# A later down product, three sums pinned to VectorE, and one level instead of two in one more chunk: an attention and expert kernel on one Trainium2 core

## The chip, the cores and the metric

The program runs on one core of a Trainium2 chip. The metric is the time of one execution on the device in microseconds; lower is better. Before the change it is 1823.2 us (median of 3 runs, 1819.77 to 1824.88). The granted clock is the share of its full clock that TensorE was given, 1.00 at most. "PE" is TensorE, "DVE" VectorE, "ACT" ScalarE, "POOL" GpSimd, "SP" the engine that issues most transfers here (580 of the 692 that the trace of the kernel before lists; POOL issues the rest).

## The reference, cut to what matters

```python
kv  = np.einsum('bhsd,bhse->bhde', k, v)            # linear attention, 8 batches, 8 heads
out = np.einsum('bhsd,bhde->bhse', q, kv)
x   = (out / rms(out) * g_norm)                     # reshaped to 4608 rows x 512
p   = probs / (probs.sum(-1, keepdims=True) + 1e-9)
for e in range(4):                                  # four experts
    h = np.maximum(x @ w1[e], 0.0)                  # "up":   512 -> 1024
    out += p[:, e:e+1] * (h @ w2[e])                # "down": 1024 -> 512
```

All in fp32. The four experts are the four passes of the kernel; each pass goes over nine chunks of 512 rows. I count passes from 0 and chunks of the whole program from 0 to 35, so chunk 9 is the first of pass 1.

## The kernel before

The products use a scheme with 7 instead of 8 block products. The up product applies it twice (7 x 7 small products of 128 columns). The down product applies it once (256 columns, `down`) or twice (128 columns, `down_deep`): fewer multiplications, but sums before and after on DVE and POOL. A planner in the kernel's own Python takes every operation with a cost it was given, a key that says how early it is wanted, and the buffers it needs, and lays down the order of each engine; the program that runs follows that order.

```python
def either(n):                       # the planner may choose DVE or POOL
    return {"DVE": 0.17 + 0.00108 * n, "POOL": 0.1 + 0.0025 * n}
...                                  # cut
SHAPE = {"big": (29, 2 * NT), ...}   # 29 buffers of 4 KB a partition, and 4 more later
...                                  # cut: in up(), as the inner products end, hidden forms h[..]
            elif m == 7:
                add(key, made[1], made[1], made[7])
                add(key, unit(4), made[1], made[5])
                relu(key, h[4])
                add(key, unit(5), h[21], h[4])
                add(key, unit(6), h[5], h[1], ALU.subtract)
...                                  # cut: up's PSUM banks are emptied by
nc.vector.tensor_tensor(out=block(whole, a, t), in0=src.ap[:, 0:HN], in1=add_.ap[:], op=ALU.add)
...                                  # cut: second-level sums of w2, 28 of 256 columns a pass
combine(deep + j / 7, either(HN), parts[o][1], parts[a][1], parts[b][1], op, ...)
...                                  # cut: down and down_deep
        h = hidden.pop(s)
        base = s + 1.0               # when the down product of chunk s is wanted
...
            if e and 1 <= c < NCH - 1:   # e: pass, c: chunk in the pass, NCH = 9
                down_deep(s, e, c)
            else:
                down(s, e, c)
```

PSUM banks are the buffers that this program's matmuls write to. In the profile, L802 is the up matmul, L966 the one-level and L1039 the two-level down matmul. L826 is the sum that empties an up bank, L1072 the same for a two-level down bank. L337 is every sum and difference from SBUF to SBUF on DVE or POOL, L1100 a sum of two-level down products, L936 the output transfer that adds into memory. "big", "small", "kv", "x_rem" and "kvbd" are names of buffers that the planner gives out; for most purposes they are one store.

## Time and profile before

| | before |
|---|---|
| median time | 1823.2 us (later rounds 1820 to 1822) |
| span in the profile | 1817.9 us |
| PE matmul instructions | 14390: 7056 up, 4116 two-level down, 1680 one-level down, rest attention |
| busy PE / DVE / POOL | 97 / 67 / 60% |

The prediction below shows the lines that carry the argument. I add two groups of L337, the 1024-column sums on DVE and on POOL (out and in shapes, count, then total busy us and mean ns):

```profile
L337 DVE TENSOR_TENSOR big<-big,big 128x1024 f32<-128x1024 f32 x238 | 340.0, 1431 | 32.7 <-ACT big L785 25.2 <-POOL big L337 1.3 <-issue 1.0
L337 POOL TENSOR_TENSOR big<-big,big 128x1024 f32<-128x1024 f32 x97 | 238.8, 2468 | 92.5 <-DVE big L826 27.4 <-PE db L966 18.2 <-ACT big L785 13.7
```

PE is the bound, so what counts is where PE does not run back to back. I measured that as a **loss**: over all neighbouring matmuls, the distance from start to start beyond 0.1116 us (128 columns) or 0.2164 us (256 columns), summed by chunk. The loss includes a lower granted clock: in the kernel before it was 0.50 from 952.2 us on for 3.41 us, and matmuls of 128 columns started 0.213 us apart there. It can be checked from a window: its length less its own matmuls. Before, chunks 8 to 35 lose 62.7 us in all.

### The profile page before, as it was taken

The page shows a single profiled execution, that of the slowest core. Times are in us where ns is not written, and L with a number is a line of the kernel's source. Part 1 is how long each engine was busy: PE and PEld are TensorE (multiplying, and loading weights), DVE is VectorE, ACT ScalarE, POOL GpSimd, SP SyncE. Part 2 cuts the span into 40 slices and gives each one's busy share as a digit, 9 for nine tenths or more (in the row PEclk, how much of TensorE's full clock was granted, in tenths as well). Part 3 has the DMA queues.
Part 4 walks back from the last instruction along what each step waited for, and adds up shares of the span by engine and source line. Part 5 has one row for each costly group of instructions (what it writes and reads, how often), then busy time and mean ns, then how long its engine had stood idle before and what let it go on. Part 6 is the DMA issues. An engine that isn't in the chain of part 4 may idle for free.

```text
span 1817.9 us, 36718 instructions
## 1 busy us (share of the span) xinstructions
PE 1764.0 (97%) x14390; PEld 1693.5 (93%) x14390; DVE 1211.4 (67%) x1929; ACT 825.7 (45%) x1961; POOL 1085.7 (60%) x898
## 2 busy tenths in 40 slices
PE   8999999999999999999989999999998999999998
PEld 8899999999999999999988899999997899999997
DVE  4755565556565667677777667777777666777774
ACT  3544444454333345554443344545443344445452
POOL 4975544546554556666565566666655756675752
PEclk9899999999999999999999999999999999999999
DMA  9844453533433444444544434444445434444442
GB/s 228 247 154 148 136 164 125 148 105 116 157 128 105 105 101 106 116 105 110 150 109 108 102 98 104 106 109 107 129 140 118 99 95 108 105 106 105 105 105 47
DMA packets 148589, 220.83 MB, mean 121 GB/s; under 512 B 49600, under 2 KB 90816, under 8 KB 148416
## 3 DMA queue, kind: packets, MB, share of 16 engines
q1 hardware_dynamic: 133312, 191.21, 33.7%
q0 software_dynamic: 15104, 27.27, 10.9%
q8 instruction: 113, 1.85, 0.4%
q14 instruction: 60, 0.49, 0.1%
HBM read 145.30 MB, written 73.14 MB: 120 GB/s over the span
## 4 chain that ended last, share of the span: by engine, by line
PE 88%; DVE 7%; issue 2%; POOL 1%; DMA 1%; ACT 0%; SPq 0%; DVEq 0%; POOLq 0%
PE u L802 41%; PE db L966 16%; PE db L1039 13%; PE ab L1039 10%; DVE big L337 4%; PE ab L966 3%; PE ab L595 1%; DVE big L1100 1%; PE ab L577 1%; DVE big L826 1%; PE ab L562 1%; PE ab L605 1%; PE u L1164 1%; DMA out_dram<-big 0%; DVE small L1100 0%
## 5 line engine op out<-in xcount | busy, mean ns | idle before, releaser
L802 PE MATMUL u<-xf,big 128*128 128x128 f32 x3456 | 481.9, 278 | 11.9 <-DVE big L337 7.2
L802 PEld LDWEIGHTS u<-xf,big 128*128 128x128 f32 x3456 | 440.8, 194 | 22.6 <-ACT snap L818 6.9
L826 DVE TENSOR_TENSOR big<-u,snap 128x256 f32<-128x256 f32 x696 | 286.7, 420 | 249.2 <-PE u L802 152.6
L337 DVE TENSOR_TENSOR big<-big,big 128x1024 f32<-128x1024 f32 (+1 forms) x359 | 425.2, 1197 | 32.7 <-ACT big L785 25.2
L818 ACT ACTIVATE snap<-u 128x256 f32<-128x256 f32 x756 | 287.9, 382 | 310.0 <-PE u L802 227.5
L337 POOL TENSOR_TENSOR big<-big,big 128x256 f32<-128x256 f32 (+1 forms) x206 | 329.8, 1610 | 152.4 <-DVE big L337 54.9
L802 PE MATMUL u<-xf,w1y 128*128 128x128 f32 x2700 | 377.5, 277 | 19.5 <-DVE big L826 15.7
L802 PEld LDWEIGHTS u<-xf,w1y 128*128 128x128 f32 x2700 | 339.8, 192 | 27.2 <-DVE big L826 20.1
L966 PE MATMUL db<-big,big 128*128 128x256 f32 x1256 | 297.3, 381 | 7.6 <-DVE big L337 7.6
L966 PEld LDWEIGHTS db<-big,big 128*128 128x128 f32 x1256 | 228.9, 191 | 34.0 <-DVE big L337 8.4
L1064 ACT ACTIVATE snap<-db 128x256 f32<-128x256 f32 x252 | 89.4, 356 | 173.6 <-PE db L1039 166.4
L337 POOL TENSOR_TENSOR big<-big 128x512 f32<-128x512 f32 (+1 forms) x91 | 142.3, 1564 | 43.0 <-ACT big L785 31.3
L936 POOL DMA_DIRECT2D out_dram<-big x102 | 91.6, 1005 | 118.9 <-ACT big L913 66.2
L785 ACT ACTIVATE big<-big 128x1024 f32<-128x1024 f32 x130 | 136.7, 1051 | 26.5 <-DVE big L337 26.4
L1072 DVE TENSOR_TENSOR big<-ab,snap 128x256 f32<-128x256 f32 (+1 forms) x216 | 82.9, 384 | 94.9 <-PE ab L1039 67.5
L818 ACT ACTIVATE big<-u 128x256 f32<-128x256 f32 x232 | 88.5, 382 | 103.7 <-PE u L802 100.6
L1039 PE MATMUL db<-big,big 128*128 128x128 f32 x820 | 113.3, 276 | 0.4 <-DVE big L337 0.4
L913 ACT ACTIVATE big<-db,p_all 128x256 f32<-128x256 f32 x88 | 41.6, 473 | 136.5 <-PE db L966 136.3
L1039 PEld LDWEIGHTS db<-big,big 128*128 128x128 f32 x820 | 102.0, 192 | 0.7 <-DVE big L337 0.6
L1039 PE MATMUL ab<-kv,big 128*128 128x128 f32 x608 | 87.2, 275 | 0.0
L1039 PE MATMUL db<-kv,big 128*128 128x128 f32 x600 | 84.8, 275 | 0.0
L920 DVE SCALAR_TENSOR_TENSOR big<-db,p_all,big 128x256 f32<-128x256 f32 x70 | 33.8, 483 | 74.6 <-PE db L966 73.3
(200 smaller groups left out, 2665.7 us busy)
## 6 DMA issues: line engine op xcount, KB each, us to landing
xf<-x SPq DMA_DIRECT2D x108, 512.0 KB, 3.6
out_dram<-big POOLq DMA_DIRECT2D x86, 256.0 KB, 5.3
xf<-x_h SPq DMA_DIRECT2D x81, 256.0 KB, 3.0
xf<-x SPq DMA_DIRECT2D x81, 256.0 KB, 3.4
x<-xf SPq DMA_DIRECT2D x36, 512.0 KB, 3.2
big<-in_moe_w_dram SPq DMA_DIRECT2D x27, 512.0 KB, 6.9
small<-in_q_dram SPq DMA_DIRECT2D x72, 128.0 KB, 3.6
kv<-in_k_dram SPq DMA_DIRECT2D x30, 288.0 KB, 3.3
```

The costliest lines, as they stand in the source:

```text
L337: lambda eng: adder(eng).tensor_tensor(out=out_(), in0=a(), in1=b(), op=op),
L785: lambda eng: nc.scalar.activation(out=b.ap[:], in_=b.ap[:], func=ACT.Relu),
L802: nc.tensor.matmul(ps.ap[:, u * P:(u + 1) * P], lhsT=w1f[e][m][mm][1]()[:, u * P:(u + 1) * P], rhs=views[m][mm][1](), start=(mm in (1, 2, ...
L818: lambda eng: nc.scalar.activation(out=where(), in_=ps.ap[:, 0:HN], func=ACT.Copy),
L826: lambda eng: nc.vector.tensor_tensor(out=block(whole, a, t), in0=src.ap[:, 0:HN], in1=add_.ap[:], op=ALU.add),
L913: lambda eng: nc.scalar.activation(out=cell(i, half), in_=ap(), func=ACT.Copy, scale=prob()),
L920: lambda eng: nc.vector.scalar_tensor_tensor(out=cell(i, half), in0=ap(), scalar=prob(), in1=cell(i, half), op0=ALU.mult, op1=ALU.add,),
L936: nc.gpsimd.dma_start(out=dst, in_=cell(i)[parts, :], accum_op=ALU.add)
L966: nc.tensor.matmul(ps.ap[:, 0:HN], lhsT=four(h[m])[:, kt // 2, t, kt % 2, :], rhs=w2f[e][m].ap[:, kt * HN:(kt + 1) * HN], start=(m in (1, ...
L1039: nc.tensor.matmul(ps.ap[:, o * P:(o + 1) * P], lhsT=b.ap[:, col:col + P], rhs=w2q[e][m][mm][1]()[:, kt, :], start=(mm in (1, 2, 5) and o ...
L1064: lambda eng: nc.scalar.activation(out=where(), in_=group_of(ps.ap), func=ACT.Copy),
L1072: lambda eng: nc.vector.tensor_tensor(out=cell(tq, dq), in0=group_of(src.ap), in1=group_of(add_.ap), op=ALU.add,),
```

## The change

Intent: give the sums between an up and its down product more time, keep the last of these sums off the slower engine (a 1024-column sum took 2.47 us on average on POOL, 1.22 undisturbed on DVE), and relieve DVE and POOL of two-level work in the last two chunks of a pass, when the next pass's weights are being summed.

```diff
-        def add(key, to, a, b, op=ALU.add):
+        def add(key, to, a, b, op=ALU.add, where=either):
...
-                add(key, unit(4), made[1], made[5])
+                add(key, unit(4), made[1], made[5], where=dve)
                 relu(key, h[4])
-                add(key, unit(5), h[21], h[4])
-                add(key, unit(6), h[5], h[1], ALU.subtract)
+                add(key, unit(5), h[21], h[4], where=dve)
+                add(key, unit(6), h[5], h[1], ALU.subtract, dve)
...
-        base = s + 1.0                       # in down and in down_deep
+        base = s + 1.2
...
-            if e and 1 <= c < NCH - 1:
+            if e and 1 <= c < NCH - 2:
```

I call the three parts the sums, the trail and the level.

More of the change, by code (lines that the diff above doesn't have):

```diff
@@ L774, in up @@
         h = {}
-        def add(key, to, a, b, op=ALU.add):
+        def add(key, to, a, b, op=ALU.add, where=either):
             combine(
-                key, either(2 * NT), lambda: to.ap[:], lambda: a.ap[:], lambda: b.ap[:], op,
+                key, where(2 * NT), lambda: to.ap[:], lambda: a.ap[:], lambda: b.ap[:], op,
                 [a, b], [to],
@@ L992, in down_deep @@
         h = hidden.pop(s)
-        base = s + 1.0
+        base = s + 1.2
         merge, send = result(s, e, c, base)
```

## The prediction

Passages of the recorded text are cut, as marked: they told of the hardware what no run here shows. No term of the forecast was in them; its sum is -22.9 us, which gives the 1800. The times in ns are those of one sum (L337).

> **What bounds the kernel now.** I read the page first, then the chain of waits, then a table of stretches cut at the chunk borders, then the timeline where that table shows lost time. The page:
>
> ```profile
> PE 1764.0 (97%) x14390; PEld 1693.5 (93%) x14390; DVE 1211.4 (67%) x1929; ACT 825.7 (45%) x1961; POOL 1085.7 (60%) x898
> ...
> PE 88%; DVE 7%; issue 2%; POOL 1%; DMA 1%; ACT 0%; SPq 0%; DVEq 0%; POOLq 0%
> ```
>
> TensorE is the bound: 97% busy, 88% of the chain. A change can win only in the 7% that the chain gives to VectorE, and must pay for every matmul it adds. To place the 7%, I cut the span where each chunk's first up product starts (196 up matmuls a chunk, 36 chunks, four passes of nine; passes counted from 0). Columns: window; its length; busy us and count of PE, PEld, DVE, ACT, POOL; granted clock; DMA share; GB/s.
>
> ```profile
> 485.60:532.10 46.50, 46.35 (x309) 43.10 (x309) 26.48 (x45) 16.99 (x39) 28.86 (x20) 1.00 0.47 156
> 532.10:579.90 47.80, 46.57 (x309) 43.31 (x308) 31.54 (x45) 17.56 (x40) 19.90 (x14) 1.00 0.33 100
> 579.90:626.70 46.80, 44.68 (x302) 41.78 (x302) 29.76 (x37) 17.67 (x41) 24.81 (x28) 1.00 0.36 96
> ```
>
> ```profile
> 671.00:714.80 43.80, 43.80 (x395) 43.80 (x394) 31.71 (x54) 22.61 (x56) 28.11 (x23) 1.00 0.41 106
> ...
> 894.00:942.60 48.60, 46.16 (x399) 45.19 (x398) 35.48 (x59) 21.40 (x54) 29.12 (x24) 1.00 0.46 136
> 942.60:999.50 56.90, 50.73 (x318) 46.30 (x317) 40.51 (x59) 21.08 (x47) 34.17 (x27) 0.97 0.49 115
> 999.50:1046.50 47.00, 44.67 (x302) 41.78 (x302) 28.50 (x38) 16.89 (x40) 27.09 (x30) 1.00 0.41 102
> ...
> 1090.40:1136.00 45.60, 44.21 (x390) 43.63 (x389) 34.28 (x55) 22.28 (x56) 30.19 (x22) 1.00 0.44 104
> 1136.00:1180.20 44.20, 44.20 (x398) 44.20 (x397) 32.33 (x55) 22.77 (x57) 28.35 (x23) 1.00 0.41 105
> ```
>
> The second fence is quoted from the stretches of passes 1 and 2; the first is the end of pass 0. In the trace, matmuls of 128 columns follow each other every 0.1116 us (1.79 us for 16), those of 256 columns every 0.2164 us (3.46 for 16). So an up product is 196 x 0.1116 = 21.9 us, a two-level down product 196 x 0.1116 = 21.9, a one-level one 112 x 0.2164 = 24.2. Whatever a window has beyond its own matmuls is lost. The loss is 0.0 in 671 to 714.8 and 2.3 in 1090 to 1136; such pairs alternate through passes 2 and 3. Around the change of weights, the three chunks from the pass's last on lose 3.5 + 10.0 + 2.5 = 16.0 us (894 to 1046.5) and the same places one pass later 16.1. The end of pass 0, where every down product is one-level already, loses 0.4 + 1.7 + 2.3 = 4.4. That contrast carries my prediction. What holds PE in the worst chunk:
>
> ```profile
> 946.73 2.58 DVE L337 TENSOR_TENSOR big<-big,big 128x1024 f32<-128x1024 f32 x1
> ...
> 952.78 1.22 DVE L337 TENSOR_TENSOR big<-big,big 128x1024 f32<-128x1024 f32 x1
> ...
> 961.35 3.15 DVE L337 TENSOR_TENSOR big<-big,big 128x1024 f32<-128x1024 f32 x1
> ```
>
> ```profile
> 943.56 4.67 POOL L337 TENSOR_TENSOR big<-big,big 128x1024 f32<-128x1024 f32 x2
> ...
> 961.06 2.36 POOL L337 TENSOR_TENSOR big<-big,big 128x1024 f32<-128x1024 f32 x1 [1.12 <-DVE big L826]
> ```
>
> The same add takes 1.22 us when POOL rests and 2.58 or 3.15 when POOL adds at that time; a PSUM bank's evacuation stands behind it, and PE needs the bank. Last, the end of the kernel:
>
> ```profile
> 1785.02 2.96 DVE big L337 x2
> 1787.98 0.04 issue
> 1788.02 12.31 PE db L966 x48
> ```
>
> The last down product needs two chained sums (its forms 5 and 6), and PE, with nothing else left, stands for 3.56 us.
>
> [...]2468 ns mean on POOL, 1216 ns undisturbed on DVE, for 1024 columns.[...] the granted clock is 0.97 in the 56.9 us chunk and 0.94 in its twin one pass later[...].
>
> **The change part by part.**
>
> (a) One level for the last-but-one chunk of passes 1 to 3. It removes 3 x 196 matmuls of 128 columns and adds 3 x 112 of 256: 3 x (24.24 - 21.87) = +7.1 us, all on the path. It removes, per chunk, for DVE and POOL together: 7 differences of 512 columns, 14 of 256, 7 sums of 512, and 9 evacuation sums of 256 with 3 of 128. At the undisturbed DVE times in the trace (0.68, 0.41, 0.68, 0.42, 0.29) that is 4.8 + 5.7 + 4.8 + 3.8 + 0.9 = 20 us. One-level output has 6 accumulating merges of 0.48 us on DVE, 2.9 us, the other 8 on ACT at 0.47 us, which has room. Net some 17 us of DVE and POOL work leave the stretch just before the weight sums of the next pass (DVE plus POOL: 64.6 us in 894 to 942.6, 74.7 in the next), and 11 of the 4 KB buffers are no longer asked for, so weights can land and be summed sooner. If passes 1 and 2 then ended like pass 0, (16.0 - 4.4) + (16.1 - 4.4) = 23.3 us would return. I count three quarters of it, 17.5, because the trailing down product keeps eight hidden forms longer just where both sets of weights need the buffers, and because the 2.5 us loss of the chunk where the second-level weights are summed stays in pass 0's case too.
>
> (b) The down product a fifth of a chunk later. It adds no instruction, and no PE time. It gives the chain behind the up outputs (sum, ReLU, sum, difference) 0.2 x 45 = 9 us more. At the end it leaves PE about 0.2 x 24.2 = 4.8 us of the former down product to do after the last up product, more than the 3.56 us hole. That last stretch also ran at a clock of 0.91 after its hole; the whole loss from 1738 us on is 5.5 us. I count 4.5 back.
>
> (c) Three sums a chunk on DVE only. Of the eleven 1024-column sums of a steady two-level chunk POOL makes 3 to 5 now; in the chunks I placed by hand, one or two of them are among these three. So about 1.5 x 1.22 = 1.8 us more DVE work a chunk of 44 (32 to 35 busy now), some 3.7 us less on POOL, and fewer collisions, unless the planner gives POOL other sums. All two-level chunks of steady state together lose 20.6 us now (5.3, 7.7 and 7.6 in passes 1 to 3). With (b) I count 8 of these, less than half: those waits are PSUM evacuations behind a sum that collided, and neither part removes the other sums on POOL.
>
> Pass 0 I leave as it is: its steady chunks are 59.6 us of back-to-back matmuls with no loss.
>
> Sum: +7.1 - 17.5 - 4.5 - 8 = -22.9 us. From 1823.2 that gives about 1800; **1800 us predicted**, 1.3% less.
>
> **The rivals.** First, the buffers: hidden forms that live longer push the weight loads later, and new waits on loads or on w1 sums take the place of the removed ones. For it: the loads already trickle in pairs between 870 and 953 us, as room comes. Against it: part (a) frees eleven. Then only the final hole is won and the net is near 0: 1818 to 1828. Second, PE pays 7.1 us and the collisions only move: the schedule is made by a planner that takes fixed durations, so each new order has its own bad coincidences. For it: the same kind of chunk loses 0.0 in one place and 2.3 in the next. Against it: pass 0's end is the same code and loses 4.4. This gives 1805 to 1815. Third, everything works: pass ends like pass 0 (-23.3), end hole closed (-5.5), steady losses down to 6 (-14.6), +7.1, so -36.3: 1787, just at the 2% line. DVE as the new bound I think unlikely: below 36 of 44 us in steady chunks.
>
> **Range and chances.** The middle of these is 1800; 8 times in 10 between 1784 and 1816. Faster by over 2% needs below 1786.7, the third rival's full size: 0.13. Slower by over 2% needs +36 us, five times the added matmuls, with a bound engine that otherwise does the same work: 0.02. Within 2%: 0.85.
>
> **What would show it.** Step (a): the windows of the last chunks of passes 1 and 2 hold 112 matmuls of 256 columns, and the chunk after loses under 5 us instead of 10, at a granted clock of 1.00; the weight loads start earlier than 870. Step (b): no wait of 3.56 us before the last down product. Step (c): no 1024-column sum of forms 4, 5, 6 on POOL, POOL busy under 1085.7 us, steady pairs of chunks under 89.8 us. I am wrong if the chunks at the change of passes still lose 8 us or more, or if steady chunks lose more than 1.1 us on average, which is what they lose now.

## The result, and the profile after

The changed kernel takes 1795.13 us (median of 4 runs, 1793.68 to 1795.63) against 1821.49 us of the kernel before in the same rounds (4 runs). The ratio is 0.9852, 95% interval 0.9834 to 0.9871. (Ratios here are the mean time of one kernel's runs over that of the other's of the same rounds, so not quite the ratio of the medians.) That is 1.5% faster; 1800 was predicted.

The page after, span, busy time and the chain by engine:

```profile
span 1793.0 us, 36253 instructions
...
PE 1760.0 (98%) x14138; PEld 1683.6 (94%) x14138; DVE 1177.1 (66%) x1909; ACT 815.9 (46%) x1913; POOL 973.0 (54%) x816
...
PE 84%; POOL 5%; DMA 5%; DVE 3%; issue 2%; ACT 1%; SPq 1%; DVEq 0%; POOLq 0%; ACTq 0%
```

DVE fell from 7 to 3% of the chain. Something new stands there: POOL and DMA, 5% each. I come back to it. The stretches after, cut the same way (window, length, busy us and count of PE, PEld, DVE, ACT, POOL, clock, DMA share, GB/s): the second chunk of pass 1 (in the second chunk of each later pass w2's second-level sums are made), the three chunks at the change from pass 1 to 2, and two steady chunks.

```profile
576.10:625.30 49.20, 46.28 (x303) 42.95 (x302) 32.00 (x46) 19.03 (x41) 27.56 (x29) 0.97 0.36 97
891.00:938.60 47.60, 46.98 (x331) 44.31 (x331) 35.62 (x57) 21.37 (x51) 24.96 (x23) 1.00 0.65 171
938.60:986.30 47.70, 47.70 (x317) 44.63 (x316) 23.40 (x37) 17.47 (x40) 28.35 (x21) 1.00 0.47 117
986.30:1035.60 49.30, 46.25 (x301) 43.12 (x301) 33.36 (x42) 18.47 (x40) 26.71 (x33) 0.97 0.37 96
1078.80:1123.90 45.10, 44.27 (x395) 43.98 (x395) 33.10 (x55) 22.94 (x57) 28.49 (x21) 1.00 0.42 106
1123.90:1168.50 44.60, 44.22 (x395) 43.94 (x394) 33.09 (x55) 22.89 (x57) 28.44 (x21) 1.00 0.45 107
```

The chunk of 56.9 us has become one of 47.7 in which PE never stops. The chunk after it, 47.0 us before, has become worse: 49.3. The two steady chunks last 89.7 us together, as good as unchanged from 89.8. The end of the kernel, in the chain:

```profile
1763.83 12.09 PE db L966 x56
1775.91 12.10 PE ab L966 x56
```

The hole of 3.56 us in front of the last down product is gone.

**The losses of all runs.** us lost on PE; "end 0" are chunks 8 to 10, "end 1" 17 to 19, "end 2" 26 to 28 (last chunk of a pass and the two after it); "border" is the sum over the third and eighth chunk of passes 1 to 3, "inner" over the four between them; "last" is chunk 35 with the tail. "Median" and ratio are timed; losses are of the one profiled run.

| kernel | median us | ratio (95%) | end 0 | end 1 | end 2 | border | inner | last |
|---|---|---|---|---|---|---|---|---|
| before | 1821 | 1 | 4.4 | 16.0 | 16.1 | 9.4 | 11.2 | 5.5 |
| the change | 1795.1 | 0.9852 (.9834-.9871) | 9.1 | 5.7 | 5.7 | 1.9 | 11.4 | 0 |
| level | 1805.2 | 0.9905 (.9889-.9922) | 6.1 | 7.9 | 6.3 | 5.9 | 11.2 | 5.8 |
| trail, passes 1-3 | 1811.6 | 0.9939 (.9919-.9959) | 2.1 | 16.1 | 15.9 | 1.4 | 14.1 | 1.0 |
| sums 4 and 6 | 1805.0 | 0.9905 (.9882-.9928) | 2.9 | 15.0 | 15.3 | 2.8 | 8.1 | 7.9 |
| trail (1-3) + level | 1804.7 | 0.9902 (.9887-.9917) | 2.0 | 11.3 | 10.2 | 4.1 | 14.4 | 0 |
| trail + sums | 1813.8 | 0.9956 (.9941-.9971) | 9.1 | 15.2 | 15.3 | 2.5 | 13.8 | 2.7 |
| level + sums 4, 6 | 1790.8 | 0.9837 (.9820-.9855) | 2.9 | 4.5 | 4.5 | 2.8 | 8.4 | 4.0 |
| the change, trail 1-3 only | 1788.6 | 0.9821 (.9803-.9839) | 1.3 | 5.5 | 5.7 | 2.2 | 12.9 | 0 |

Kernels with the level have 7.1 us more matmul in them, which no column shows.

How far does one profiled run fix a loss? The kernel before and the one with the level alone have the same order of instructions on PE, DVE, ACT and POOL up to 879 us. Yet chunk 10 loses 2.3 us in the first and 4.0 in the second. Both have the same wait of 2.1 us there; the granted clock over the chunk was 0.96 in the second run and 1.00 in the first, with 46.28 and 44.68 us of busy PE. So a difference of less than 2 us in one place says nothing by itself. The profiled run of the trail alone was also the fastest of its four (1806.7 us, median 1811.6), so its losses are on the low side.

### The profile page after: what moved, and what is told of

It reads as the page before. It is cut to its first block, busy times and chain, and to the rows that moved or that the text cites. A ratio compares the mean times of both kernels' runs of the same rounds, so it can differ in the third digit from the quotient of the medians.

```text
span 1793.0 us, 36253 instructions
## 1 busy us (share of the span) xinstructions
PE 1760.0 (98%) x14138; PEld 1683.6 (94%) x14138; DVE 1177.1 (66%) x1909; ACT 815.9 (46%) x1913; POOL 973.0 (54%) x816
## 4 chain that ended last, share of the span: by engine, by line
PE 84%; POOL 5%; DMA 5%; DVE 3%; issue 2%; ACT 1%; SPq 1%; DVEq 0%; POOLq 0%; ACTq 0%
PE u L802 38%; PE db L966 18%; PE db L1039 9%; PE ab L1039 8%; PE ab L966 6%; DMA out_dram<-big 4%; POOL big L337 4%; DVE big L337 2%; PE ab L595 1%; PE ab L577 1%; POOL out_dram L936 1%; PE ab L605 1%; PE ab L562 1%; SPq L343 1%; DVE big L1072 1%
## 5 line engine op out<-in xcount | busy, mean ns | idle before, releaser
L826 DVE TENSOR_TENSOR big<-u,snap 128x256 f32<-128x256 f32 x675 | 280.6, 422 | 305.6 <-PE u L802 201.7
L802 PEld LDWEIGHTS u<-xf,big 128*128 128x128 f32 x3600 | 456.9, 192 | 9.3 <-ACT snap L818 1.2
L337 POOL TENSOR_TENSOR big<-big,big 128x256 f32<-128x256 f32 (+1 forms) x181 | 295.8, 1638 | 206.5 <-DVE big L337 107.8
L337 DVE TENSOR_TENSOR big<-big,big 128x1024 f32<-128x1024 f32 (+1 forms) x330 | 379.1, 1160 | 32.1 <-ACT big L785 14.5
L802 PE MATMUL u<-xf,w1y 128*128 128x128 f32 x2700 | 381.1, 277 | 11.5 <-DVE big L826 10.3
L966 PE MATMUL db<-big,big 128*128 128x256 f32 x1336 | 316.8, 381 | 0.0
L966 PEld LDWEIGHTS db<-big,big 128*128 128x128 f32 x1336 | 242.4, 191 | 26.8
L785 ACT ACTIVATE big<-big 128x1024 f32<-128x1024 f32 x130 | 136.6, 1052 | 20.6 <-DVE big L337 18.1
L1072 DVE TENSOR_TENSOR big<-ab,snap 128x256 f32<-128x256 f32 (+1 forms) x204 | 78.8, 386 | 70.9 <-PE ab L1039 40.3
L337 POOL TENSOR_TENSOR big<-big 128x512 f32<-128x512 f32 (+1 forms) x53 | 74.5, 1406 | 44.5 <-ACT big L785 23.2
L1100 POOL TENSOR_TENSOR big<-big 128x512 f32<-128x512 f32 x17 | 36.2, 2131 | 113.2 <-ACT snap L818 113.2
L337 DVE TENSOR_TENSOR big<-big 128x512 f32<-128x512 f32 (+1 forms) x70 | 93.7, 1342 | 0.2 <-POOL big L337 0.2
L1039 PE MATMUL db<-big,big 128*128 128x128 f32 x648 | 89.8, 275 | 0.0
L966 PE MATMUL ab<-big,big 128*128 128x256 f32 x360 | 85.8, 384 | 0.0
```

The costliest lines, as they stand in the source:

```text
L337: lambda eng: adder(eng).tensor_tensor(out=out_(), in0=a(), in1=b(), op=op),
L785: lambda eng: nc.scalar.activation(out=b.ap[:], in_=b.ap[:], func=ACT.Relu),
L802: nc.tensor.matmul(ps.ap[:, u * P:(u + 1) * P], lhsT=w1f[e][m][mm][1]()[:, u * P:(u + 1) * P], rhs=views[m][mm][1](), start=(mm in (1, 2, ...
L826: lambda eng: nc.vector.tensor_tensor(out=block(whole, a, t), in0=src.ap[:, 0:HN], in1=add_.ap[:], op=ALU.add),
L966: nc.tensor.matmul(ps.ap[:, 0:HN], lhsT=four(h[m])[:, kt // 2, t, kt % 2, :], rhs=w2f[e][m].ap[:, kt * HN:(kt + 1) * HN], start=(m in (1, ...
L1039: nc.tensor.matmul(ps.ap[:, o * P:(o + 1) * P], lhsT=b.ap[:, col:col + P], rhs=w2q[e][m][mm][1]()[:, kt, :], start=(mm in (1, 2, 5) and o ...
```

## The experiments

Theory A was the prediction's: the level cures the ends of passes, the trail closes the last hole, sums and trail help the steady chunks. Rival B: the trail cures the ends of passes. Rival C, the prediction's first: buffers held longer turn into new waits.

A part of the field can't be tried. With the trail of 1.2 in all passes alone, or with the level, or all three sums at a trail of 1.0, the planner stops: no operation can start, with several kinds of buffers down to none free. So the trail alone was tried in passes 1 to 3, and two of the three sums alone.

### One level alone

```diff
-            if e and 1 <= c < NCH - 1:
+            if e and 1 <= c < NCH - 2:
```

> One level in the last-but-one chunk alone (trail 1.0, sums as before). Theory A, that the pass ends recover because the differences and sums of the two-level product are gone from DVE and POOL: the chunks around the change of weights lose 5 to 6 us instead of 16, twice, for 7.1 us more matmul; the 3.6 us hole before the last down product stays or shrinks little; steady chunks still lose about 1.1 us each. Some 1808 to 1812, ratio 0.993. Rival B, that the later trail makes the pass ends good: the loss of about 16 us stays and the time is 1825 to 1829, ratio 1.003.

Measured: 1805.23 us, ratio 0.9905, a little better than expected. The ends of passes 1 and 2, last chunk and the next:

```profile
893.60:945.60 52.00, 50.15 (x323) 46.67 (x322) 38.07 (x55) 19.86 (x44) 24.96 (x23) 0.97 0.55 150
945.60:994.70 49.10, 46.52 (x309) 43.28 (x308) 29.35 (x42) 18.13 (x40) 23.69 (x22) 1.00 0.38 99
```

DVE in the chunk after the change of weights has 29.35 us of work against 40.51 before, and the chunk 49.1 us against 56.9. The losses of 16 us fall to 7.9 and 6.3; the last hole stays (5.8). Theory A holds for this part, rival B falls.

What PE waited for in the chunk of 56.9 us before (total us, times, longest) tells more:

```profile
PE u L802 <- DVE big L337: 3.2, 2, 2.1
PE db L966 <- DVE big L337: 1.4, 1, 1.4
PE u L802 <- DVE big L826: 0.9, 1, 0.9
```

An up product reads no hidden form, so the sum of L337 that it waits for in the first line is one of the new weights. This wait stands in the traces of all four kernels that keep two levels at the ends of passes 1 and 2 (whole run: before 7.2 us, trail 10.6, trail and sums 5.0, sums 4.7), and in none of the ten with one level there. In the kernel before, the last load of the new weights is issued at 952.9 us, 10 us into that chunk; with the level alone it is issued at 935.4, 10 us before the same chunk begins. So less work for DVE and POOL and buffers free sooner both fit; no run separates them.

### The trail alone, in passes 1 to 3

```diff
-        base = s + 1.0
+        base = s + (1.2 if e else 1.0)        # in down and in down_deep
```

> Trail 1.2 alone, in passes 1 to 3 (in pass 0 as well the planner finds no order: the buffers run out). Theory A: only the end hole closes (5 us) and the steady chunks gain 3 to 8, the pass ends stay near 16 us lost or get worse since hidden forms hold buffers longer: 1808 to 1818, ratio 0.994 to 1.0. Rival B: the pass ends recover too, 1795 to 1800, ratio 0.987.

Measured: 1811.56 us, ratio 0.9939. The chunk after the change of weights, of the same kind as the 56.9 us one:

```profile
932.80:991.80 59.00, 50.24 (x322) 45.82 (x321) 44.83 (x61) 20.82 (x49) 29.89 (x23) 0.94 0.43 106
```

It is longer than before, DVE is busier in it (44.83 us against 40.51) and the granted clock is lower (0.94 against 0.97); the ends of passes lose 16.1 and 15.9 us. The last hole shrinks to 1.0. So far theory A. Not foreseen: the border chunks gain 8 us (9.4 to 1.4) while the inner ones lose 2.9 more (11.2 to 14.1).

### Trail and level

> Trail 1.2 in passes 1 to 3 and one level in the last-but-one chunks, but sums 4, 5 and 6 free to go to POOL. If the DVE-only sums matter little by themselves: within 4 us of the full change, 1793 to 1800, ratio 0.986. If they carry the steady chunks: 1802 or more, ratio over 0.989.

The edit is both of the above. Measured: 1804.66 us, ratio 0.9902, no better than the level alone, though the last hole is closed. It is the second branch of the expectation: without the sums the full change's time is not reached. The full change has its later trail in pass 0 too; the fair comparison is the change with the trail in passes 1 to 3 only (below, ratio 0.9821). Against that the sums are worth some 15 us: 10.3 us of loss at the ends of passes 1 and 2, and 3.4 in border and inner chunks. So they carry not so much the steady chunks: the loss at the ends of passes moved one chunk on, to the second chunk of the next pass:

```profile
983.40:1036.80 53.40, 47.48 (x301) 43.93 (x300) 31.97 (x40) 18.05 (x40) 29.19 (x33) 0.94 0.35 88
```

That is the chunk in which the 28 second-level sums of w2 are made. It loses 9.1 us here, 2.5 before, 4.9 in the full change.

### Trail and sums, two levels kept

> Trail 1.2 in all passes and the three sums on DVE alone, two levels up to the last chunk but one as before. Theory A: the pass ends lose 12 us or more each, the end hole is closed, steady chunks lose about 0.7: 1805 to 1815, ratio 0.994. Rival B: as good as the full change or better by the 7 us of matmul that it doesn't add: 1788 to 1795, ratio 0.983.

The edit is the full change without its last two lines. Measured: 1813.82 us, ratio 0.9956. The ends of passes 1 and 2 still lose 15.2 and 15.3 us. Rival B is out for good: neither trail nor sums cure the ends. Of the last hole 2.7 us are left, where I had expected it closed.

### Two of the sums alone

```diff
-                add(key, unit(4), made[1], made[5])
+                add(key, unit(4), made[1], made[5], where=dve)
-                add(key, unit(6), h[5], h[1], ALU.subtract)
+                add(key, unit(6), h[5], h[1], ALU.subtract, dve)
```

> Two of the three sums (forms 4 and 6) on DVE alone, nothing else (all three alone find no order in the planner). Theory: by themselves they do little, since other sums stay on POOL: 1815 to 1822, ratio 0.998, steady chunks 0.7 to 1.1 us lost, pass ends still 15 us, end hole down by 1 to 2 us as form 4 takes 1.2 instead of 2.35 us. Rival: they are what makes steady chunks good, 0.993.

Measured: 1805.04 us, ratio 0.9905. I had expected them to do little, and they do as much as the level: the rival in the expectation was right. Two steady chunks:

```profile
1084.50:1128.50 44.00, 44.00 (x394) 43.86 (x393) 34.61 (x62) 22.74 (x56) 23.62 (x18) 1.00 0.43 107
1128.50:1172.90 44.40, 44.05 (x390) 43.54 (x389) 35.95 (x50) 22.66 (x56) 29.25 (x26) 1.00 0.44 107
```

They last 88.4 us against 89.8 before, with DVE at 34.6 and 36.0 us instead of 34.3 and 32.3 and POOL at 23.6 and 29.3 instead of 30.2 and 28.4: three and two 1024-column sums on POOL where there were five and three. Inner chunks fall from 11.2 to 8.1 us lost, border from 9.4 to 2.8, end 0 from 4.4 to 2.9. The last hole did not shrink, it grew (7.9); that part of the expectation was wrong as well.

### Level and two sums: the change without its trail

> One level in the last-but-one chunks and sums 4 and 6 on DVE alone, trail 1.0 as before: the change without its trail. If one level (17 us alone) and the sums (17 us alone) work in different places, the pass ends and the steady chunks, they add up to 34 us: 1786 to 1791, ratio 0.982, with the end hole of 3.6 us or more still there, and the trail is worth only that hole. If the trail is needed for the steady chunks: 1797 or more, ratio over 0.987.

The edit is the level's and the two sums' together. Measured: 1790.8 us, ratio 0.9837. The interval (0.9820 to 0.9855) overlaps that of the full change (0.9834 to 0.9871), so the two are not told apart, but a benefit of the trail (and of the third sum, which can't be separated here) can't be seen: what it wins at the end (4.0 us here) it loses elsewhere. The two gains add up nearly (0.9905 x 0.9905 = 0.981).

### The full change with the old trail in pass 0

```diff
-        base = s + 1.2
+        base = s + (1.2 if e else 1.0)        # in down and in down_deep
```

> The full change with the trail of 1.0 in pass 0 (so all three parts, trail in passes 1 to 3 only). If the 9.1 us that the end of pass 0 loses in the full change (4.4 before, 2.0 with trail and level in later passes) come from the longer trail in pass 0: 5 to 8 us faster than the full change, 1787 to 1791, ratio 0.981. If they come from the DVE-only sums: the same as the full change, 0.985.

Measured: 1788.57 us, ratio 0.9821; its interval ends at 0.9839, just inside that of the full change, the medians lie 6.6 us apart. End 0 falls from 9.1 to 1.3 us. So the trail in pass 0 costs what was expected, and the sums pinned to DVE are not to blame. Of the 7.8 us, 4.8 lie in chunk 10, and the next experiment takes these away with the trail left as it is (end 0: 4.2).

### w2's second-level sums on DVE alone

In the full change the second chunks of passes 1 to 3 lose 4.8 to 4.9 us each. The chain there:

```profile
993.46 6.81 DVE big L337
1000.26 0.68 DVE big L826 x2
1000.94 0.04 issue
1000.98 2.01 PE u L802 x8
```

The 1024-column add takes 6.81 us instead of 1.22. POOL's timeline at that time, first and last of the run:

```profile
993.13 1.29 POOL L337 TENSOR_TENSOR kv<-big,kv 128x256 f32<-128x256 f32 x1
993.98 1.13 POOL L337 TENSOR_TENSOR kv<-kv,big 128x256 f32<-128x256 f32 x1
994.66 1.12 POOL L337 TENSOR_TENSOR x_rem<-small 128x256 f32<-128x256 f32 x1
...
998.08 1.09 POOL L337 TENSOR_TENSOR x_rem<-small,x_rem 128x256 f32<-128x256 f32 x1
```

Eight POOL sums follow each other without a gap, and two bank evacuations and PE stand behind the DVE add. The add ends 1.10 us after the last POOL sum does, and the two long adds in the prediction's fences (from 946.73 and 961.35) end 1.08 us after the POOL sum beside them. Undisturbed it takes 1.22 us in all. So these three adds were held up until POOL had finished, not slowed down beside it.

```diff
-                        deep + j / 7, either(HN), parts[o][1], parts[a][1], parts[b][1], op,
+                        deep + j / 7, dve(HN), parts[o][1], parts[a][1], parts[b][1], op,
```

> The full change, and the 28 second-level weight sums of w2 (256 columns, made in the second chunk of passes 1 to 3, mostly on POOL in a run without a gap) on DVE alone. Theory: the add that stood 6.8 us behind that run takes 1.2 us, the second chunk's loss of 4.9 us falls to under 1.5 us in three places, though DVE has 28 x 0.41 = 11 us more: 1784 to 1788, ratio 0.980 to 0.982. Rival: DVE has no room and the loss stays, 1793 or more.

Measured: 1789.57 us, ratio 0.9828, a little short of what was expected; the interval (0.9811 to 0.9845) overlaps that of the full change. The chunk itself is as expected, with no loss left:

```profile
985.80:1031.80 46.00, 46.00 (x310) 43.17 (x309) 33.06 (x66) 18.95 (x42) 12.18 (x12) 1.00 0.41 104
```

In the three places 4.8 + 4.9 + 4.9 us are gone, but border and inner chunks lose 6.8 + 14.7 us instead of 1.9 + 11.4: a new order, with other coincidences. So the mechanism is shown, and more than half of its gain is given back elsewhere.

### Both of the last two

> Both of the former: trail 1.0 in pass 0, and w2's second-level sums on DVE. If the two gains are separate places: end of pass 0 at 2 us, second chunks under 1.5, so 1780 to 1785, ratio 0.978.

Measured: 1785.39 us, ratio 0.9803 (0.9786 to 0.9819), just above the 1780 to 1785 us that were expected. The ends lose 1.3, 0.7 and 0.7 us; border and inner still 6.5 and 14.3.

### The differences of the two-level down product on DVE too

After those runs I took this for the cause of the inner loss: each steady chunk has one 512-column difference on DVE that takes 4.2 us instead of 0.7, as here in the full change:

```profile
1228.27 4.19 DVE L337 TENSOR_TENSOR big<-big 128x512 f32<-128x512 f32 x1
```

The edit, on top of the last kernel:

```diff
-                    at - 0.3, either(NT), lambda t=t: two(t.ap[:, 0:NT]),
+                    at - 0.3, dve(NT), lambda t=t: two(t.ap[:, 0:NT]),
-                        at - 0.29, either(HN), lambda t=t, to=to: quarter(t, to),
+                        at - 0.29, dve(HN), lambda t=t, to=to: quarter(t, to),
```

> Trail 1.0 in pass 0, w2's second-level sums on DVE, and now the 21 differences that each two-level down product makes of its hidden forms on DVE alone too. Theory: each steady chunk has one 512-column add on DVE that takes 4.2 us instead of 0.7 beside POOL's work, and PE loses 0.8 us; with these differences gone from POOL the 4.2 us add is gone and steady chunks lose 0.2 instead of 1.2, 15 x 0.8 = some 12 us: 1772 to 1778, ratio 0.974. Rival: DVE, now with some 6 us more own work a chunk, becomes the wait, and the time is 1784 to 1792.

Measured: 1818.3 us, ratio 0.999: my expectation failed, and the rival's time is passed too. SBUF sums of over 3.5 us on DVE went from 18 in the full change to 3, yet the inner chunks lose 33.3 us. But the run is not the test that I meant it to be: the planner gave POOL other work, 170 of L337's 1024-column sums in place of 102 in the kernel that this one starts from. So POOL was not out of DVE's way, and the theory is neither shown nor refuted. Who PE waits for in four steady chunks of this run (total us, times, longest):

```profile
PE ab L1039 <- DVE big L1072: 5.1, 4, 2.5
PE u L802 <- DVE small L826: 1.0, 1, 1.0
```

So I went back to the full change and asked the chain what stands in front of its inner loss, the wait of 0.6 us at 1236.8 us:

```profile
1225.42 2.36 POOL big L337
1227.79 0.52 POOL out_dram L936
1228.31 6.63 DMA out_dram<-big
...
1235.07 0.42 DVE big L1072
1235.49 0.93 DVE big L337 x2
1236.42 0.35 DVE big L1072
1236.77 0.04 issue
1236.81 1.16 PE ab L1039 x8
```

It is a buffer. The same chain, with a POOL sum of 2.4 us and a transfer of 6.4 to 6.9 us, stands in each of the four steady chunks of pass 2 that are looked at here (transfers from 1093.62, 1138.66, 1183.24 and 1228.31 us). The evacuation of a two-level down bank (L1072) may not write before an output transfer has left the buffer it was given; the transfer, 6.63 us from issue to landing, is issued by POOL behind a 1024-column sum of 2.36 us. By the waits of each whole run, DVE's L1072 waits so for "big" 13 times, 16.3 us, in the full change, 12 times, 17.3 us, with the trail alone, once, 4.6 us, before, and never in the change without its trail. Over all runs: 10 to 13 times in the eight kernels with the later trail and these differences left free, once or never in the four with the old trail, never in the two with the differences on DVE. In the four steady chunks PE waited 2.7 us for L826 before and waits 2.7 us for L1072 now, so the equal loss of the inner chunks (11.2 and 11.4) hides an exchange. That is rival C, and it is also the 5% DMA and 5% POOL in the chain of the changed kernel. That the trail brings these waits is shown by the counts. The remedy (one more buffer, or the transfers issued by another engine): that it would help is not shown. Why DVE falls behind in the last experiment is not settled: it is 69% busy, and POOL's added sums are a likely part of it.

### Two levels in the last pass

No weights follow the last pass, so its last chunk but one may keep two levels. On top of the kernel with both improvements (not of the failed one):

```diff
-            if e and 1 <= c < NCH - 2:
+            if e and 1 <= c < NCH - (2 if e < E - 1 else 1):
```

> As the kernel with trail 1.0 in pass 0 and w2's second-level sums on DVE (1785 us), but the last pass keeps two levels in its last chunk but one, since no weights follow it. If the trail alone closes the end hole (it left 1.0 us of it): 2.4 us less matmul and 1 us more loss, 1783 to 1785, ratio 0.979. If one level is needed there: hole of 3 us and colder clock, 1786 to 1789.

Measured: 1781.81 us, ratio 0.9791 (0.9776 to 0.9805), a little better than expected: the hole at the end is back with 2.7 us, but inner chunks lost 10.5 instead of 14.3, and 2.4 us of matmul are saved. The "colder clock" of the expectation is that of the kernel before, granted 0.91 from 1785 us on, where its 3.56 us hole lies; here the last 79.4 us were granted 1.00. **This is the fastest kernel**, 2.1% faster than before, though its interval still touches 2%, and better than the changed one by 0.6%: its interval lies below that of the change.

With the differences on DVE added:

> Both of the former together: if each does what it should, 1771 to 1776, ratio 0.973; if DVE is full, the end hole grows and it is 1785 or more.

Measured: 1823.36 us, ratio 1.0021, the second branch of the expectation.

## Why the prediction was right, and where it wasn't

The time, 1795.1, lies 5 us from the predicted 1800, and the sum holds by its terms. In the span of the two profiles (24.9 us less):

| term | predicted | measured |
|---|---|---|
| added matmul | +7.1 | +7.1 (252 matmuls fewer in all: 588 out, 336 in) |
| ends of passes 1 and 2 | -17.5 | -20.7 (32.1 to 11.4) |
| last hole | -4.5 | -5.5 |
| steady chunks, border and inner | -8 | -7.3 (20.6 to 13.3) |
| end of pass 0 | 0 | +4.7 (4.4 to 9.1) |
| start and rest of pass 0 | 0 | -2.6 |

The terms give -24.3; 0.6 us of the span's 24.9 are in none of them, and the start alone varies by 2.6 us between the runs, so its term means little. That the sum comes so close is in part luck: the 4.7 us at the end of pass 0 that I had not foreseen are made up by 3.2 us more than predicted at the other ends, 1.0 more at the last hole and the 2.6 of the start.

**Step (a) held, but for a reading and a sign.** The contrast that carried it, pass 0's good end against the bad ends of passes 1 and 2, was the right one: the level alone takes 18 of the 32 us away, trail and sums without it 2. In the worst chunk I read that PE waits for a bank's evacuation behind a delayed sum. That was the lesser part: 0.9 us of its waits ended so (and 0.5 with an evacuation on ACT), 3.2 with a sum of the new weights and 1.4 with a sum that a down product reads. The remedy was the same, as it makes these sums come sooner. One sign that I had named was wrong: the weight loads do not start earlier. They start at 886.7 us, before at 870.1; they come closer together and the last is issued at 940.9 instead of 952.9.

**Step (b) was right at the end and wrong about its price.** Most of the hole is closed by the trail (1.0 us with the trail alone, 5.8 with the level alone), all of it only with the level in the last pass: 2.7 us are left with trail and sums, and where the last pass keeps two levels. But "I count 8 of these" gave trail and sums together a gain in the steady chunks, and "Pass 0 I leave as it is" gave the trail no cost there. Measured, the trail alone adds 2.9 us of loss to the inner chunks of the profiled run, through buffers held by transfers, and costs 7.8 us of loss at the end of pass 0 (6.6 us of the time). "It adds no instruction, and no PE time" was true and not enough: it adds life to buffers.

**Step (c) was right in size and wrong in place.** All of the steady gain lies in the border chunks (9.4 to 1.9); the four inner chunks of each pass are where they were (11.2 and 11.4). By themselves the sums win 3.1 there; in the full change the trail eats that. And two of the three sums alone bring 17 us of time, where I had counted 8 for sums and trail together. Of the signs I named, POOL's busy time fell (1085.7 to 973.0), but "steady pairs of chunks under 89.8 us" is met by a hair, 89.7, and inner chunks lose 0.95 us on average, hardly under the 1.1 that I gave as the mark for all steady ones. DVE did not get busier either (33.1 us in steady chunks, 32.3 and 34.3 before): the planner gave POOL other sums in place of the three.

**The rivals.** The third, "everything works: 1787", is what one gets without the trail in pass 0 (1788.6) and, with the sums on DVE and two levels kept in the last pass, less (1781.8). The first, buffers, was real though not where I had looked: not in the weight loads but in the inner chunks. The second, that every new order brings its own bad coincidences, is seen in each experiment; it makes effects of one to five us hard to add up.

## What to carry to other kernels

When one place in a profile shows the good case of the same code (here the end of the one pass without two levels), its difference to the bad place is worth more than a sum of instruction times: here it gave 23.3 us, of which 17.5 were counted and 20.7 came. Delaying work by a fraction of a stage cost no engine time here, but it lengthened the life of buffers; look for who will be handed the buffer next. And look for long runs of small sums without gaps on GpSimd: here one held up a VectorE add for over 5 us (6.81 instead of 1.22). Last, a planner that may choose the engine will fill what an edit frees, so count what each engine got before reading an experiment.
